# A 64-row last slot in two column halves of the array, and a scatter and a row request that come sooner

## The chip, the cores and the metric

The kernel runs on one core of one Trainium2 chip. The metric is the device time of one execution in microseconds (us), lower is better; the time shown for a kernel is the median of its timed runs. A profiled execution gives the trace from which the rows below come. "PE" is TensorE, "PEld" its weight loads, "DVE" VectorE, "ACT" ScalarE, "POOL" GpSimd, "SP" SyncE, which here issues nearly all transfers; a "q" behind a name (SPq, PEq) means the engine's sequencer.

## The reference

Sliding-window attention over q, k, v of shape 8 x 8 x 576 x 64 (batch, head, position, depth) with a window of 64, and behind it a mixture of 8 experts over the 4608 resulting rows of 512 numbers, each row going to the one expert that its logits choose:

```
scores = where(0 <= i - j < 64, q @ k.T / 8, -1e9);  x = softmax(scores) @ v      # per batch and head
logits = x @ w_gate + modality_bias[modality_id];    e = argmax(logits)            # per row, 8 experts
gate   = softmax(logits)[e]
out[row] = gate * (relu(x[row] @ w1[e]) @ w2[e])                                    # w1: 512x1024, w2: 1024x512
```

The inputs are float32. With the data of the benchmark three experts get rows: 1841, 2289 and 478.

## The kernel before

**Attention.** The 4608 rows are 36 pairs of two 64-row blocks. A loop over steps `s` runs four stages on different pairs: scores of pair `s` (64x64 tiles of the array, float32), the minima that mask and reduce them on DVE (`minima`, eight instructions with eight reads of the accumulator), exponentials on ACT (`exps`, split in groups of heads), transposes of the probabilities of pair `s-1` (`probs_t`), values of pair `s-2` (`values`, each float32 matmul a column half of the array: outputs on partitions 0 to 63 and 64 to 127), logits of pair `s-3`. The result of a pair goes into one of five buffers `xa` (512 numbers, the gate, the row's number). Transposes of q and k for the next group `G` of two pairs run in `part(0)` and `part(1)`; for some groups the upper four heads are loaded as 32x32 pieces (32x8x32 transfers) and turned on DVE instead of PE. DVE, ACT, POOL, SP and PE all execute in program order; the order is written out by hand.

**Routing.** Every second step a group's rows get a place in the scratch table `xs_scratch` in DRAM (`route1` to `route3`), in small DVE operations that wait in a list `routing` and are emitted a few at a time by `tick`. From group 4 on the last part (a cast of the indices, and per pair a copy of the row numbers on POOL and an indirect scatter of `xa`) is kept in `held` and emitted one step later by `release()`, which first empties `routing`.

**Experts.** Rows are worked off in slots of 256 rows of one expert. `slot_pieces` yields a slot in 16 pieces, and in the attention from step `FIRST` = 12 on each step interleaves four pieces (`gap`); behind the attention the pieces follow one another. A slot: `fetch` asks SP for the rows (`load_slot`, five transfers into the single buffer `xt`; SP waits there for the scatters that the slot needs), `x_turn` transposes them in 32x32 blocks on DVE, `x_part` splits each number into two reduced-precision parts (`xh`, `xl`), `first` makes the hidden layer from 3 products per term (`Whi*xh`, `Wlo*xh`, `Whi*xl`), `second` the output in the same way, `finish` multiplies by the gate and scatters the rows to `out`. Weights of an expert come in 16 pieces of 128x512 and are split into `Whi` (ACT) and `Wlo` (DVE).

**The end.** 18 whole slots are followed by one of at most 128 rows (one expert has 49 rows left over): `half_first` twice (12 matmuls of 512 columns each, 3 products), a transposition of the hidden layer and a split (`half_turn`) twice, `half_second` twice (24 matmuls of 256 columns each), with the last output pieces of the slot before in between. Then the two halves of its output are multiplied by the gate and scattered.

Of the kernel before, what the change touches and what calls it, by code (L numbers as in the profile page):

```python
# [19 lines left out]
P = 128  # L20
W64 = 64
# [5 lines left out]
def tile_window_attn_moe(  # L27
# [100 lines left out]

    def tick(n=1, table=False):
        for _ in range(n):  # L130
            if routing and not table:
                routing.pop(0)()
            elif queue:
                queue.pop(0)()
                issued[0] += 1
# [67 lines left out]
    def load_slot(row_ap, late, nb):  # L203
# [5 lines left out]
        parts.append((tail_of(xt)[:, 0:nb], rows[:, :, DM:ROW].rearrange("b p c -> p b c")))  # L209
        for dst, src in parts:  # L210
# [17 lines left out]

    todo = []
# [31 lines left out]
    def x_turn(sl):  # L261

        nb = sl["nb"]
        flat = sl["xt"].rearrange("p b c -> p (b c)")
        for b in range(nb):
            nc.vector.transpose(out=flat[:, b * DM:(b + 1) * DM], in_=flat[:, b * DM:(b + 1) * DM])  # L266

    def slot_pieces():


        def x_part(sl, i):

            xt, nb = sl["xt"], sl["nb"]
            if i == 0:
                sl["x"] = [epool.tile([P, NC1 * TP], F32R, name=nm) for nm in ("xh", "xl")]
                if nb == 1:
                    return
            cs_ = slice(2 * i, 2 * i + 2) if nb == 2 else slice(0, NC1)
            raw = x_of(xt)[:, 0:nb].rearrange("p b w c t -> p c (b w) t")[:, cs_]
            hi, lo = (x[:, cs_.start * nb * P:][:, 0:512].rearrange("p (c w t) -> p c w t", w=nb * NR, t=R32)  # L280
                      for x in sl["x"])

            def out_():
                split(raw, hi, lo)
                if i == 1:
                    sl["gate"] = epool.tile([P, 2], F32, name="gate", bufs=2)
                    nc.gpsimd.tensor_copy(out=sl["gate"][:, 0:nb], in_=tail_of(xt)[:, 0:nb, 0])
                    sl["id"] = epool.tile([P, 2], I32, name="id", bufs=2)
                    nc.gpsimd.tensor_copy(out=sl["id"][:, 0:nb], in_=tail_of(xt)[:, 0:nb, 1])
# [53 lines left out]
        def half_first(sl, n):  # L343

            buf = sl["buf"]
            hb = bank(n)
            hi, lo = sl["x"]
            mm = [(x, w, c) for c in range(NC1) for x, w in ((hi, Whi), (hi, Wlo), (lo, Whi))]
            for m, (x, w, c) in enumerate(mm):
                c0 = c * F + n * 512  # L350
                ready(sl, c0)
                nc.tensor.matmul(  # L352
                    out=hb, lhsT=x[:, c * P:(c + 1) * P], rhs=w[buf][:, c0:c0 + 512],
                    start=(m == 0), stop=(m == len(mm) - 1))
            hs = sl["hs", n] = work.tile([P, HP, P], F32, name="ss", bufs=3)
# [3 lines left out]
        def half_turn(sl, n):  # L359
            tp = bank(2)  # L360
            for c in range(HP):
                turn(tp[:, c * P:(c + 1) * P], sl["hs", n][:, c, :])
            hh = epool.tile([P, 512], F32R, name="hh", bufs=2)
            hl = epool.tile([P, 512], F32R, name="hl", bufs=2)
            sl["h", n] = hh, hl
            later.append(lambda: split(tp, hh, hl))

        def half_second(sl, a):

            buf = sl["buf"]  # L370
            cols = slice(a * DM // 2, (a + 1) * DM // 2)
            yp = ps_m.tile([P, DM], F32, name=f"y{a}")
            mm = [(w, n, c, lo) for n in range(2) for c in range(HP) for w, lo in ((Whi, 0), (Wlo, 0), (Whi, 1))]
            for m, (w, n, c, lo) in enumerate(mm):
                c0 = WC + (n * HP + c) * DM
                ready(sl, c0)
                nc.tensor.matmul(  # L377
                    out=yp[:, cols], lhsT=sl["h", n][lo][:, c * P:(c + 1) * P],
                    rhs=w[buf][:, c0 + cols.start:c0 + cols.stop],
                    start=(m == 0), stop=(m == len(mm) - 1))  # L380
            id2 = epool.tile([P, 1], I32, name=f"id{a}")
            nc.gpsimd.tensor_scalar(
                out=id2, in0=tail_of(sl["xt"])[:, 0, 1:2], scalar1=2.0, scalar2=float(a),
                op0=ALU.mult, op1=ALU.add)

            def out_():
                y = epool.tile([P, DM], F32, name="y", bufs=4)
                nc.vector.tensor_scalar(
                    out=y[:, 0:DM // 2], in0=yp[:, cols], scalar1=sl["gate"][:, 0:1], scalar2=None, op0=ALU.mult)
# [19 lines left out]
        while True:  # L409
            nxt = None  # L410
            for k in range(1, NK):
                for i in range(2):
                    if k == 1 and i == 0 and last:
                        nxt = fetch()
                        turn_at = 0
                    first(sl, k, i)
                    if k == NK - 1 and i == turn_at:
                        later.append(lambda: x_turn(nxt))
                    yield
                for t in range(2):  # L420
                    if k == 2 and t == 1 and nxt is None:
                        nxt = fetch()
                        turn_at = 1
                    second(sl, k - 1, t)
                    if k == NK - 1 and nxt and t == 1:
                        x_part(nxt, 1)
                    yield
                    if k == NK - 1 and nxt and t == 0:
                        x_part(nxt, 0)
                        run_later()  # L430
            second(sl, NK - 1, 0)
            yield
            if nxt["nb"] == 1:
                break
# [7 lines left out]
        half_first(nxt, 0)  # L442
        yield
        half_first(nxt, 1)
        yield
        half_turn(nxt, 0)
# [3 lines left out]
        half_turn(nxt, 1)  # L450
        yield
        half_second(nxt, 0)
        yield
        half_second(nxt, 1)
# [55 lines left out]
    QUARTERS = 8  # L510
# [42 lines left out]
    def quartered(G):  # L553

        return G >= QUARTERS and GBLK * G // BPB == (GBLK * G + GBLK - 1) // BPB

# [4 lines left out]
    def by_heads(t):  # L561
# [891 lines left out]
```

## Time and profile before

| | us |
|---|---|
| median of 3 timed runs | 620.34 (619.72 to 621.35) |
| profiled execution, its own time | 618.77 |
| its span, first to last instruction | 617.0 |
| PE busy | 596.8 |
| DVE busy | 389.0 |
| ACT busy | 292.7 |
| POOL busy | 139.2 |

The span is what the trace covers; the profiled execution's own time has 1.77 us around it. Its mean granted TensorE clock is 0.996 of full speed. "Busy" is the union of an engine's instructions; matmuls are pipelined, so their recorded durations overlap and the distance of two starts is what one costs.

### The profile page before, as it was taken

What the parts mean: (1) busy time and instruction counts of PE and PEld (TensorE: products, weight loads), DVE (VectorE), ACT (ScalarE), POOL (GpSimd) and SP (SyncE); (2) the same over time, 40 slices, a digit from 0 to 9 for tenths busy, and PEclk for the clock granted to TensorE, in tenths of its full rate; (3) what the DMA queues carried; (4) which work ended last, traced back from release to release, by engine and by line L of the source; (5) the groups of instructions that cost most, each with busy time, mean ns of one, the idle gap of its engine ahead of it and who ended that gap; (6) DMA issues with size and microseconds to landing.
All of it is one profiled execution on the core that took longest, in us unless ns stands there. A gap on an engine that the chain in (4) does not pass through costs nothing.

```text
span 617.0 us, 17344 instructions
## 1 busy us (share of the span) xinstructions
PE 596.8 (97%) x6309; PEld 534.2 (87%) x6309; DVE 389.0 (63%) x1493; ACT 292.7 (47%) x926; POOL 139.2 (23%) x315
## 2 busy tenths in 40 slices
PE   6999889999999999999999999999999999999996
PEld 4888778879898888988888899999999989999986
DVE  4899988877777877678655464323323834776622
ACT  3999885665656564646462111111112513554411
POOL 6323322132312311321223131001001101101202
PEclk9999999999999999999999999999999999999999
DMA  9989866685766745564413035522234534678300
GB/s 165 207 217 256 215 177 173 155 204 130 191 164 165 202 104 126 138 142 88 117 52 105 35 102 172 173 70 69 78 127 124 166 123 137 196 252 253 103 17 21
DMA packets 175111, 88.08 MB, mean 143 GB/s; under 512 B 138746, under 2 KB 157744, under 8 KB 174896
## 3 DMA queue, kind: packets, MB, share of 16 engines
q1 hardware_dynamic: 166400, 67.46, 44.8%
q0 software_dynamic: 5888, 18.93, 8.3%
q8 instruction: 50, 0.82, 0.6%
q10 hardware_dynamic: 2736, 0.58, 0.5%
q14 instruction: 37, 0.30, 0.2%
HBM read 67.49 MB, written 23.91 MB: 148 GB/s over the span
## 4 chain that ended last, share of the span: by engine, by line
PE 77%; DVE 5%; ACT 2%; issue 1%; DMA 1%; SPq 0%; POOL 0%; POOLq 0%; DVEq 0%; ACTq 0%
PE y L326 29%; PE em L304 21%; PE sp L304 10%; PE tp L470 7%; PE av L696 3%; PE sp L640 3%; PE tp L725 1%; DVE xt L266 1%; PE y L377 1%; DVE ss L654 1%; ACT ss L666 1%; DVE xl L196 1%; DMA xs_scratch<-xa,idx 1%; PE sp L352 0%; PE em L352 0%
## 5 line engine op out<-in xcount | busy, mean ns | idle before, releaser
L326 PE MATMUL y<-Whi,hh 128*128 128x512 f32 x288 | 115.7, 402 | 0.0
L666 ACT ACTIVATE ss<-ss,mn 128x128 f32<-128x128 f32 x288 | 112.3, 398 | 4.6 <-DVE less L159 3.7
L326 PE MATMUL y<-Wlo,hh 128*128 128x512 f32 x288 | 112.7, 391 | 0.0
L326 PE MATMUL y<-Whi,hl 128*128 128x512 f32 x288 | 112.4, 390 | 0.0
L337 POOL DMA_INDIRECT out_dram<-y,id x36 | 39.8, 1104 | 223.5 <-DVE y L334 161.3
L313 DVE SCALAR_TENSOR_TENSOR hl<-em,hh 128x512 fp32r<-128x512 f32 x50 | 34.5, 691 | 81.2 <-ACT hh L312 74.8
L304 PE MATMUL em<-xh,Whi 128*128 128x256 f32 x400 | 82.0, 286 | 0.0
L304 PE MATMUL em<-xh,Wlo 128*128 128x256 f32 x400 | 79.1, 279 | 0.0
L304 PE MATMUL em<-xl,Whi 128*128 128x256 f32 x400 | 79.1, 279 | 0.0
L312 ACT ACTIVATE hh<-em 128x512 fp32r<-128x512 f32 x50 | 29.9, 599 | 100.3 <-PE em L304 81.0
L675 ACT COPY pT<-tp 128x512 f32<-128x512 f32 x57 | 31.3, 589 | 78.6 <-PE tp L470 77.8
L654 DVE CUSTOM_DVE_ANT_0 ss<-sp,masks 128x128 f32<-128x128 f32 x288 | 63.6, 286 | 2.9 <-PE sp L640 2.0
L304 PEld LDWEIGHTS em<-xh,Whi 128*128 128x128 f32 x400 | 62.8, 188 | 2.6 <-issue 0.2
L326 PEld LDWEIGHTS y<-Whi,hl 128*128 128x128 f32 x288 | 54.1, 188 | 12.1
L326 PEld LDWEIGHTS y<-Whi,hh 128*128 128x128 f32 x288 | 54.1, 188 | 8.8
L326 PEld LDWEIGHTS y<-Wlo,hh 128*128 128x128 f32 x288 | 54.2, 188 | 8.5
L304 PEld LDWEIGHTS em<-xl,Whi 128*128 128x128 f32 x400 | 60.9, 188 | 0.0
L304 PEld LDWEIGHTS em<-xh,Wlo 128*128 128x128 f32 x400 | 60.9, 188 | 0.0
L809 POOL DMA_INDIRECT xs_scratch<-xa,idx x36 | 36.3, 1009 | 90.7 <-DVE e_n_p L154 30.6
L666 ACT ACTIVATION_READ_ACCUMULATOR ss<-ss,mn 128x1 f32 x288 | 56.1, 195 | 0.0
L312 ACT ACTIVATE hh<-sp 128x512 fp32r<-128x512 f32 x22 | 13.1, 597 | 76.2 <-PE sp L304 72.2
L696 PEld LDWEIGHTS av<-ve,pT 128*64 128x64 f32 x576 | 36.3, 138 | 12.6 <-issue 8.1
(242 smaller groups left out, 1194.4 us busy)
## 6 DMA issues: line engine op xcount, KB each, us to landing
xt<-xs_scratch SPq DMA_DIRECT2D x72, 128.0 KB
vo<-in_v_dram SPq DMA_DIRECT2D x32, 256.0 KB
y<-in_moe_w_dram SPq DMA_DIRECT2D x32, 256.0 KB
vo<-in_moe_w_dram SPq DMA_DIRECT2D x24, 256.0 KB
ss<-in_moe_w_dram SPq DMA_DIRECT2D x24, 256.0 KB
xs_scratch<-xs_scratch SPq DMA_DIRECT2D x8, 514.0 KB
pT<-in_moe_w_dram SPq DMA_DIRECT2D x16, 256.0 KB
qk<-in_k_dram SPq DMA_DIRECT2D x22, 128.0 KB
```

What stands on the lines that cost most here:

```text
L304: nc.tensor.matmul(out=hb[:, i * TP:(i + 1) * TP], lhsT=w[buf][:, c0:c0 + P], rhs=x[:, c * TP:(c + 1) * TP], start=(n == 0), stop=(n == le ...
L312: nc.scalar.activation(out=hh, in_=hb, func=AF.Relu),
L313: nc.vector.scalar_tensor_tensor(out=hl, in0=hb, scalar=0.0, in1=hh.bitcast(F32), op0=ALU.max, op1=ALU.subtract)))
L326: nc.tensor.matmul(out=sl["y", t], lhsT=h[:, i * TP + t * P:i * TP + (t + 1) * P], rhs=w[buf][:, c0:c0 + DM], start=(k == 0 and n == 0), s ...
L337: ins = nc.gpsimd.indirect_dma_start(out=out, out_offset=bass.IndirectOffsetOnAxis(ap=sl["id"][:, t:t + 1], axis=0), in_=y, in_offset=None ...
L470: nc.tensor.transpose(out=out_, in_=in_, identity=ident[p0:p0 + n, p0:p0 + n])
L640: nc.tensor.matmul(out=sp[a][c * W64:(c + 1) * W64, hp * P:(hp + 1) * P], lhsT=qT[rows, place(g + c, hp), :], rhs=kT[rows, win(c, hp), :], ...
L654: nc.vector.tensor_tensor_reduce(out=ss[a][:, hp, :], in0=sp[a][:, hp * P:(hp + 1) * P], in1=mask, scale=-1.0 / 8.0, scalar=3.0e38, op0=AL ...
L666: nc.scalar.activation(out=ss[a][:, hp, :], in_=ss[a][:, hp, :], func=AF.Exp, bias=mn[:, h:h + 1], scale=-1.0, accum_out=sm[:, h:h + 1])
L675: nc.scalar.copy(out=pT, in_=pp)
L696: nc.tensor.matmul(out=by_block(av)[c * W64:(c + 1) * W64, a, :, hp, :], lhsT=pT[:, i:i + W64], rhs=(vo if c else ve)[p][:, 2 * hp + a, :] ...
L809: ins = nc.gpsimd.indirect_dma_start(out=xs, out_offset=bass.IndirectOffsetOnAxis(ap=idx[:, j:j + 1], axis=0), in_=xg[j], in_offset=None)
```

## The change

The core of the diff:

```diff
@@ half slot @@
-        def half_first(sl, n):            # 12 matmuls of 128x512: x parts against Whi, Wlo
+        def half_first(sl):
+            hb = sl["hb"] = bank(0)
+            x = sl["xt"].rearrange("p b c -> p (b c)")
+            for c in range(NC1):
+                for n in range(2):
+                    c0 = c * F + n * 512
+                    nc.tensor.matmul(
+                        out=hb[n * W64:(n + 1) * W64], lhsT=x[:, c * W64:(c + 1) * W64], rhs=plain_w[c0 // WCH],
+                        start=(c == 0), stop=(c == NC1 - 1))
+        def half_second(sl):
+            yp = bank(2)[:, 0:DM // 2]
+            for m in range(NC2):
+                c, n = divmod(m, 2)
+                for a in range(2):
+                    c0 = WC + (n * HP + c) * DM
+                    nc.tensor.matmul(
+                        out=yp[a * W64:(a + 1) * W64], lhsT=sl["h"][:, c, n * W64:(n + 1) * W64],
+                        rhs=plain_w[c0 // WCH][:, a * DM // 2:(a + 1) * DM // 2], start=(m == 0), stop=(m == NC2 - 1))
@@ order of the end @@
-        half_first(nxt, 0); half_first(nxt, 1); half_turn(nxt, 0); second(sl, NK - 1, 1)
-        half_turn(nxt, 1); half_second(nxt, 0); half_second(nxt, 1)
+        half_first(nxt); second(sl, NK - 1, 0); half_turn(nxt); second(sl, NK - 1, 1); half_second(nxt)
@@ a slot's rows, in the attention @@
-                    if k == 2 and t == 1 and nxt is None:     # before second(sl, 1, 1)
-                        nxt = fetch()
-                        turn_at = 1
+                    if (k, i) == ((1, 0) if last else (2, 1)) and nxt is None:   # before first(sl, 2, 1)
+                        nxt = fetch()
-                    if k == NK - 1 and i == turn_at:
+                    if k == NK - 1 and i == 0:
                         later.append(lambda: x_turn(nxt))
@@ values_out @@
+        nc.gpsimd.tensor_copy(out=xa[:, DM + 1:DM + 2], in_=idc[:, p:p + 1])
@@ scatter @@
-            nc.gpsimd.tensor_copy(out=xg[j][:, DM + 1:DM + 2], in_=idc[:, p:p + 1])
+            nc.gpsimd.memset(pause, 0.0)
             ins = nc.gpsimd.indirect_dma_start(
@@ release @@
         if held:
-            tick(len(routing))
-            held.pop(0)()
+            ready_at, rows = held.pop(0)
+            assert done_routing[0] >= ready_at
+            rows()
@@ main loop @@
             minima(s)
+            if s > FIRST:
+                release()
...
             run_later()
-            release()
             tick(2)
...
-            for f, args in at.pop(s, ()):
-                f(*args)
+            loads(3)
...                                   # loads(1) behind part(0), loads(1) behind part(1), loads(9) at the end
```

The last slot holds at most 64 rows (the expert for it must have an odd number of 64-row blocks left). Its rows lie once per column half; its weights are loaded whole into 16 buffers of the finished attention (`plain_w`: `qT`, `xa`, `qk`, `ve`, `xaT`) and aren't split. `half_turn` transposes both halves at once, and its result goes to SBUF by a copy on ACT and one on DVE of 256 columns each. In the attention the transfers of q and k for one group are given out in parts over a step (`loads`), the plain heads first, the 32x8x32 ones later; which heads are loaded in which form stays as it was. From step 13 on, the held scatter stands directly behind the minima, and the rest of `routing` is no longer emptied there.

PE, at the end of the program (`em`, `sp`, `tp` and `y` are PSUM banks, `Whi`, `Wlo` the weight parts, `hh`, `hl` and `ss` the hidden layer). Before, from the last matmul of the second `half_first` into the first `half_second`:

```order
3227 L352 MATMUL sp_9459<-Whi_2524,xl 128x512
3228 L470 MATMUL tp<-ident_r,ss 128x128 x4
3229 L326 MATMUL y_9334<-Whi_65,hh 128x512
3230 L326 MATMUL y_9334<-Wlo_66,hh 128x512
3231 L326 MATMUL y_9334<-Whi_65,hl 128x512
3232 L326 MATMUL y_9334<-Whi_65,hh 128x512
3233 L326 MATMUL y_9334<-Wlo_66,hh 128x512
3234 L326 MATMUL y_9334<-Whi_65,hl 128x512
3235 L470 MATMUL tp<-ident_r,ss 128x128 x4
3236 L377 MATMUL y_9504<-Whi_2524,hh 128x256
3237 L377 MATMUL y_9504<-Wlo_67,hh 128x256
3238 L377 MATMUL y_9504<-Whi_2524,hl 128x256
```

The same place in the changed kernel, down to the last matmul:

```order
3208 L339 MATMUL y_9330<-Whi_65,hl 128x512
3209 L475 MATMUL tp<-ident_r,ss 128x128 x4
3210 L339 MATMUL y_9337<-Whi_65,hh 128x512
3211 L339 MATMUL y_9337<-Wlo_66,hh 128x512
3212 L339 MATMUL y_9337<-Whi_65,hl 128x512
3213 L339 MATMUL y_9337<-Whi_65,hh 128x512
3214 L339 MATMUL y_9337<-Wlo_66,hh 128x512
3215 L339 MATMUL y_9337<-Whi_65,hl 128x512
3216 L389 MATMUL tp<-xa_105,ss 64x256 x2
3217 L389 MATMUL tp<-qk,ss 64x256 x8
3218 L389 MATMUL tp<-ve,ss 64x256 x4
3219 L389 MATMUL tp<-xaT,ss 64x256 x2
```

24 matmuls of 128x512 (L352), 48 of 128x256 (L377) and 4 transposes are gone; 8 of 64x512 (L364, ahead of the output pieces shown) and 16 of 64x256 (L389) stand instead. Everywhere else PE's order is unchanged.

POOL, at steps 13 and 14 (`ve` and `rs` serve the values of a later step; `xa<-idc` is the copy of row numbers; the first scatter that is held). Before:

```order
103 L537 COPY ve<-vo 64x512
104 L681 TENSOR_SCALAR rs<-sm 128x8
105 L808 COPY xa_104<-idc 128x1
106 L809 DMA xs_scratch<-xa_104,idx 39168x514
107 L808 COPY xa_105<-idc 128x1
108 L809 DMA xs_scratch<-xa_105,idx 39168x514
109 L537 COPY ve<-vo 64x512
110 L681 TENSOR_SCALAR rs<-sm 128x8
```

Changed:

```order
113 L543 COPY ve<-vo 64x512
114 L692 TENSOR_SCALAR rs<-sm 128x8
115 L718 COPY xa_103<-idc 128x1
116 L819 MEMSET pause 1x1
117 L820 DMA xs_scratch<-xa_104,idx 39168x514
118 L819 MEMSET pause 1x1
119 L820 DMA xs_scratch<-xa_105,idx 39168x514
120 L543 COPY ve<-vo 64x512
121 L692 TENSOR_SCALAR rs<-sm 128x8
```

The copies of row numbers stand at the values of each step now, and a one-element memset stands ahead of each scatter.

DVE, at step 15, behind the minima (`xt` are the next slot's rows, `tgt` and `se` routing, `qT` the turned q, `hl` the hidden layer). Before:

```order
474 L543 COPY ve<-vo 64x512
475 L119 TENSOR_TENSOR Wlo_66<-y,Whi_65 128x512
476 L790 TENSOR_TENSOR tgt<-tp,ebase 128x16
477 L605 COPY qT<-tp 128x2x2x128
478 L313 SCALAR_TENSOR_TENSOR hl<-em,hh 128x512
479 L266 STREAM_TRANSPOSE xt<-xt 128x512 x2
480 L795 TENSOR_REDUCE se<-ex 128x2
```

Changed:

```order
474 L549 COPY ve<-vo 64x512
475 L279 STREAM_TRANSPOSE xt<-xt 128x512 x2
476 L119 TENSOR_TENSOR Wlo_66<-y,Whi_65 128x512
477 L802 TENSOR_TENSOR tgt<-tp,ebase 128x16
478 L616 COPY qT<-tp 128x2x2x128
479 L326 SCALAR_TENSOR_TENSOR hl<-em,hh 128x512
480 L807 TENSOR_REDUCE se<-ex 128x2
```

The two transposes of `xt` move ahead of four other operations. In step 14 the cast `idx<-dst` moves in the same way, from behind `ve` and six routing operations to directly behind the minima; ACT's small exponential of the routing (`ex`) moves behind three of the step's exponentials and the copy `xaT`. On SP, the request for `xt` moves ahead of the eight 32x8x32 transfers of q and of one or two weight transfers of its step.

## Rows read from the trace of the kernel before

**Rows 1.** The page: busy time of the engines (us, share of the span, instructions), and the granted TensorE clock in 40 slices of the span.

```profile
PE 596.8 (97%) x6309; PEld 534.2 (87%) x6309; DVE 389.0 (63%) x1493; ACT 292.7 (47%) x926; POOL 139.2 (23%) x315
PEclk9999999999999999999999999999999999999999
```

**Rows 2.** The waits of PE: line, who was waited for, us in total, times, longest.

```profile
PE tp L470 <- ACT pT L675: 3.1, 2, 1.9
PE av L696 <- POOL ve L537: 2.0, 4, 0.8
PE tp L470 <- DVE lg L730: 1.3, 3, 0.5
...
PE tp L470 <- ACT xaT L717: 0.4, 2, 0.2
```

**Rows 3.** The chain of work that ended last, from 594 us on: start, us, what.

```profile
594.07 4.11 PE y L326 x18
598.19 2.79 PE em L352 x12
600.98 2.79 PE sp L352 x12
603.78 0.44 PE tp L470 x4
604.21 1.40 PE y L326 x6
605.61 0.44 PE tp L470 x4
606.05 5.75 PE y L377 x48
611.83 0.50 DVE y L388
```

**Rows 4.** Timeline of PE where the values of one step begin and end (float32, column halves of 64): start, recorded us, line, operation, out<-moving,stationary, array rows*columns.

```profile
303.63 0.39 PE L326 MATMUL y<-Whi,hl 128*128 128x512 f32 x1
303.95 0.27 PE L696 MATMUL av<-ve,pT 128*64 128x64 f32 x1
...
304.06 0.22 PE L696 MATMUL av<-ve,pT 128*64 128x64 f32 x1
304.06 0.22 PE L696 MATMUL av<-vo,pT 128*64 128x64 f32 x1
304.11 0.22 PE L696 MATMUL av<-ve,pT 128*64 128x64 f32 x1
...
304.88 0.22 PE L696 MATMUL av<-vo,pT 128*64 128x64 f32 x1
```

**Rows 5.** Groups by line, weight loads: busy us, mean ns of one.

```profile
L326 PEld LDWEIGHTS y<-Wlo,hh 128*128 128x128 f32 x288 | 54.2, 188 | 8.5
L696 PEld LDWEIGHTS av<-vo,pT 128*64 128x64 f32 x576 | 36.3, 138 | 0.0
```

**Rows 6.** Busy time of each engine in stretches: the attention ahead of the slots, and the slots behind the attention (us, instructions; then clock, DMA share, GB/s).

```profile
15.00:72.00 57.00, 52.39 (x1006) 47.06 (x1003) 51.91 (x286) 53.56 (x213) 20.91 (x40) 0.98 0.95 225
334.00:596.00 262.00, 261.99 (x1717) 238.24 (x1718) 127.22 (x271) 74.68 (x136) 36.10 (x78) 1.00 0.42 130
```

**Rows 7.** Timelines of DVE, POOL and ACT: an output scatter that has a memset ahead of it, a held scatter that has a copy ahead of it, and the first copy of the last slot's hidden layer.

```profile
598.23 0.75 DVE L334 TENSOR_SCALAR y<-y,gate 128x512 f32<-128x512 f32 x1 [2.19 <-PE y L326]
...
599.26 0.99 POOL L337 DMA_INDIRECT out_dram<-y,id  x1 [13.67 <-DVE y L334]
...
101.21 0.16 DVE L821 CAST idx<-dst 128x2 int32<-128x2 f32 x1
...
102.15 1.06 POOL L809 DMA_INDIRECT xs_scratch<-xa,idx  x1 [7.60 <-DVE Wlo L119]
...
103.69 0.97 POOL L809 DMA_INDIRECT xs_scratch<-xa,idx  x1 [0.28 <-issue]
...
601.02 0.60 ACT L356 ACTIVATE ss<-em 128x512 f32<-128x512 f32 x1 [5.80 <-PE em L352]
```

**Rows 8.** Timelines of POOL and PE around 43 us: the copy `ve` behind a pair of scatters, and the values that wait for it.

```profile
43.02 0.62 POOL L537 COPY ve<-vo 64x512 f32<-64x512 f32 x1
...
43.70 0.27 PE L696 MATMUL av<-ve,pT 128*64 128x64 f32 x1 [0.75 <-POOL ve L537]
```

**Rows 9.** Steps 14 and 15: the scatter and the row request as pieces of the chain (start, us, what), and SP's queue (start, us to issue).

```profile
103.69 4.12 DMA xs_scratch<-xa,idx
...
110.89 1.86 DMA xt<-xs_scratch
...
97.79 5.07 SPq L590 DMA_DIRECT2D qk<-in_q_dram  x8
...
108.35 2.95 SPq L211 DMA_DIRECT2D xt<-xs_scratch  x5
```

**Rows 10.** Timelines of DVE and PE from step 14 to 16.

```profile
99.64 0.42 DVE L543 COPY ve<-vo 64x512 f32<-64x512 f32 x1
...
109.86 0.42 DVE L543 COPY ve<-vo 64x512 f32<-64x512 f32 x1
...
111.71 0.17 DVE L790 TENSOR_TENSOR tgt<-tp,ebase 128x16 f32<-128x16 f32 x1 [0.71 <-PE tp L780]
...
113.99 1.30 DVE L266 STREAM_TRANSPOSE xt<-xt 128x512 f32<-128x512 f32 x2
...
116.30 0.71 DVE L568 STREAM_TRANSPOSE qT<-qk 128x512 f32<-128x512 f32 x1
...
118.92 0.66 PE L470 MATMUL tp<-ident_r,ss 128*128 128x128 f32 x4 [0.45 <-DVE lg L730]
```

**Rows 11.** Timelines of ACT and PE: at step 20 the routing's exponential and the wait of a transpose, and behind "..." a wait of PE near the end of the attention.

```profile
165.32 0.22 ACT L756 ACTIVATE ex<-lg 128x16 f32<-128x16 f32 x1 [2.00 <-DVE lg L753]
...
167.22 0.66 PE L470 MATMUL tp<-ident_r,qk 128*128 128x128 f32 x4 [0.22 <-ACT xaT L717]
...
325.75 0.66 PE L470 MATMUL tp<-ident_r,ss 128*128 128x128 f32 x4 [0.40 <-DVE lg L730]
```

More of the change, by code (lines that the diff above doesn't have):

```diff
@@ L341, in finish @@
             tc.add_to_no_dep_group("outs", ins.ins)
-        def half_first(sl, n):
[L345 to L355, printed above, removed]
+        def half_first(sl):
[4 more added lines that the diff above has]
+                    c0 = c * F + n * 512
+                    ready(sl, c0)
+                    nc.tensor.matmul(
+                        out=hb[n * W64:(n + 1) * W64], lhsT=x[:, c * W64:(c + 1) * W64], rhs=plain_w[c0 // WCH],
+                        start=(c == 0), stop=(c == NC1 - 1))
+            hs = sl["hs"] = work.tile([P, HP, P], F32, name="ss", bufs=3)
@@ L368, in half_second @@
[L368 to L381, printed above, removed]
+                turn(tp[:, c * P:(c + 1) * P], sl["hs"][:, c, :])
@@ new lines, in half_turn @@
+            hT = sl["h"] = work.tile([P, HP, P], F32, name="ss", bufs=3)
+            flat = hT.rearrange("p c f -> p (c f)")
+            later.append(lambda: (
+                nc.scalar.copy(out=flat[:, 0:TP], in_=tp[:, 0:TP]),
+                nc.vector.tensor_copy(out=flat[:, TP:2 * TP], in_=tp[:, TP:2 * TP])))
+        def half_second(sl):
[4 more added lines that the diff above has]
+                    c0 = WC + (n * HP + c) * DM
+                    ready(sl, c0)
+                    nc.tensor.matmul(
+                        out=yp[a * W64:(a + 1) * W64], lhsT=sl["h"][:, c, n * W64:(n + 1) * W64],
+                        rhs=plain_w[c0 // WCH][:, a * DM // 2:(a + 1) * DM // 2], start=(m == 0), stop=(m == NC2 - 1))
+            id2 = epool.tile([P, 1], I32, name="id0")
+            upper = epool.tile([P, 1], F32, name="upper")
@@ L589, in load_qk @@
                     src = x[b, h, g * W64:(g + n) * W64, c * R32:(c + 1) * R32]
-                    dma.dma_start(out=by_heads(t)[rows, (h - nh) // 2, u, :],
-                                  in_=src.rearrange("(u p) d -> p u d", p=R32))
+                    other = nh == 0 and h % 2 and c
+                    (nc.scalar if other else dma).dma_start(
+                        out=by_heads(t, nh)[rows, (h - nh) // 2, u, :],
+                        in_=src.rearrange("(u p) d -> p u d", p=R32))
             i += n
     def heads_t(G, nm, i, tp):
-        src = plain(qk[G, nm], HP if quartered(G) else H).rearrange("p t (h a) d -> p t h (a d)", a=2)
+        src = plain(qk[G, nm], n_plain(G)).rearrange("p t (h a) d -> p t h (a d)", a=2)
         for h in range(2):
@@ L770, in route2 @@
     def route2(G, tp):
-        while routing:
-            routing.pop(0)()
+        tick(len(routing))
         oh = chosen[G]
@@ L824, in rows @@
             scattered.append(f"scatter_after_{G}")
-        (held if G >= HOLD else routing).append(rows)
+        if G >= HOLD:
+            held.append((done_routing[0] + len(routing), rows))
+        else:
+            routing.append(rows)
     def counts(G, tp):
@@ L898, in tile_window_attn_moe @@
             when(step, new_qk, G, nm)
-            when(step, load_qk, G, nm)
+            for h in (0, *range(max(n_plain(G), 2), H, 2)) if n_plain(G) < H else (0,):
+                when(step, load_qk, G, nm, range(GBLK), nc.sync, range(h, h + 2))
     pieces = []
@@ L1069, in tile_window_attn_moe, with loads @@
         R = (s - 5) // GB if s >= 5 and j == 1 else -1
+        def loads(n):
+            for f, args in at.get(s, [])[:n]:
+                f(*args)
+            at[s] = at.get(s, [])[n:]
         def part(i):
@@ L1158, in tile_window_attn_moe @@
             tick(n_tick)
+            loads(1)
             if s < NPR:
@@ L1167, in tile_window_attn_moe @@
         tick(n_tick)
+        if s > FIRST:
+            loads(1)
         if s == WEIGHTS:
@@ L1171, in tile_window_attn_moe @@
             weights(s)
+        if s > FIRST:
+            loads(9)
         if n_gap > 3:
@@ L1301, in tile_window_attn_moe @@
     ahead = []
+    flat = qT.rearrange("p c i -> p (c i)")
+    plain_w.extend(flat[:, n * WCH:(n + 1) * WCH] for n in range(4))
+    plain_w.extend(x[:, 0:WCH] for x in xas)
+    for _ in range(2):
+        t = work.tile([P, 2, H, D], F32, name="qk", bufs=2).rearrange("p t h d -> p (t h d)")
+        plain_w.extend(t[:, n * WCH:(n + 1) * WCH] for n in range(2))
+        plain_w.append(work.tile([P, H, D], F32, name="ve", bufs=2).rearrange("p h d -> p (h d)"))
+    plain_w.append(work.tile([P, DM], F32, name="xaT"))
+    assert len(plain_w) == 2 * WC // WCH
     waited = 0
@@ L1321, in tile_window_attn_moe @@
         if swaps and swaps[0][0] <= t:
-            swaps.pop(0)
-            split_hi(*ahead[0])
-            split_lo(*ahead.pop(0))
-    assert not swaps and not todo
+            x = swaps.pop(0)[2]
+            raw, buf, c = ahead.pop(0)
+            if x == NANY:
+                load_piece(plain_w[c], ea[x], c)
+            else:
+                split_hi(raw, buf, c)
+                split_lo(raw, buf, c)
+    assert not swaps and not todo and not held
     manual.__exit__(None, None, None)
```

102 lines of the change are left out of this document (58 added, 44 removed).

## The prediction

> **What bounds the kernel now.** I read the page first: PE is busy 596.8 of 617.0 us, no other engine above 63%, and its granted clock has a 9 in every slice [rows 1]. So only what PE executes, and the 20 us in which it stands, can shorten the run. The waits of PE say who it stood for [rows 2]: a few short ones each for ACT, POOL and DVE. The busy times by stretch say where [rows 6]: behind the attention (334 to 596) PE has 261.99 of 262.00 us, so there nothing but removed matmul time counts; from 15 to 72, ahead of the slots, it has 52.39 of 57.00, with ACT at 53.56, DVE at 51.91 and the transfer engines at 0.95. Last the chain: from 594 us on it is PE alone until 611.80, then the last output's multiplication, its scatter and the end of the program, about 5.2 us [rows 3]. These stay as they are.
>
> **The end.** Removed from the chain are the two first halves, 2.79 + 2.79, one of two turns, 0.44, and the second half, 5.75 [rows 3]: 11.77 us. The output pieces (1.40 each) and one turn remain. Added are 8 matmuls of 64x512 and 16 of 64x256 in full precision. No row before has this shape. The nearest are the values `av`: full precision, moving data 64 columns wide, outputs in two column halves. A float32 matmul is two passes there (16 matmuls of a step leave 32 records: 576 + 576 in 36 steps [rows 5]). A pass of the upper half starts with one of the lower half, both at 304.06, and from there to 304.88 the pairs follow every 0.82 / 14 = 0.0586 us (16 pairs, the first of them at 303.95) [rows 4]. In proportion, 512 columns are 0.469 us a pair. The first layer has 16 passes, 8 pairs: 3.75 us; the second 32 passes of 256, 16 pairs at 0.234: 3.75 us. Together 7.5, an upper end if some of the 0.0586 is the same for any width. The nearest wide row is a reduced-precision pass, 2.79 / 12 = 0.2325 us for 512 columns [rows 3]; two of its kind would be 0.465, the same price, and if a tenth of the 0.0586 were fixed (an estimate), some 6.8 would be the lower end. I take 7.2. Each change between the whole array and halves costs something: a last whole matmul of 512 columns at 303.63 is followed by `av` after 0.32 us instead of 0.233 [rows 4], so 0.09, three times: 0.27. The end gains 11.77 - 7.2 - 0.27 = **4.3** (4.0 to 4.7).
>
> What covers the rest of it: the first Relu, 0.60 us on ACT [rows 7], runs beside the output pieces of 1.40 that stand between the first layer and the turn. The two copies behind the turn (256 columns each) run beside the next 1.40; DVE's stands behind a multiplication `y` of 0.75 [rows 7] and so just fits. Without this cover some 0.5 us would show. The splits of the last weights, gone from ACT and DVE, gain nothing, as PE stands 0.01 us in that stretch [rows 6]; so do the ten row transfers in place of five, which are asked a slot ahead. The whole copies of the weights need buffers of the finished attention and arrive during that stretch too, where the transfer engines have a share of 0.42 [rows 6].
>
> **The steps with slots.** Here PE stands 0.45 at 118.92 for `lg` [rows 10], 0.22 at 167.22 and once more (0.4 in two) for ACT's `xaT` [rows 2, 11], and 0.40 at 325.75 for `lg` [rows 11]: 1.27 together. For `xaT` the cause is in the rows: ACT stood 2.00 us in the routing's exponential `ex`, which waits for DVE's logits [rows 11], and `xaT` was queued behind it. The change puts `ex` behind `xaT`. For `lg` DVE's order is the cause: in step 15 it did `Wlo`, `tgt`, `hl` and the 1.30 of the `xt` transposes late, from 113.99 to 115.29, then `qT` at 116.30 [rows 10]. Now the transposes come directly behind `ve`.
>
> Does `xt` arrive by then? Before, the cast of the indices ended at 101.37 and a scatter started at 102.15, with 0.78 between for the copy and a semaphore; the second started at 103.69, landed 4.12 later, SP issued the rows from 108.35 over 2.95, and the last landed at 112.75 [rows 7, 9]. Now the cast stands behind the minima, at about 99.7, where `ve` was (99.64 [rows 10]). With a memset ahead, a scatter starts 0.28 behind what it waited for (598.23 + 0.75 to 599.26 [rows 7]). So the first starts at 100.1 to 100.5, the second 1.3 to 1.5 later, 101.4 to 102.0, about 2 us sooner, and the last row lands at about 110.5 to 111.1. DVE reaches the transposes at 109.86 + 0.42 = 110.28 [rows 10]: it waits 0.2 to 0.8. Queued behind are `Wlo`, `tgt`, `qT` and `hl`, but DVE had a hole of 0.71 ahead of `tgt` [rows 10], which takes this up. What is late next is q: its eight 32x8x32 transfers, 5.07 of SP's time [rows 9], now go out behind `xt`, until about 114.5, and the last should land some 1.86 later (as `xt` [rows 9]) at 116.4, against 116.30, when DVE turned `qT` [rows 10]. So part of the 0.45 may stay. POOL's `ve` and `rs` stand behind both scatters, and are done by about 104, a step ahead of the values that need them. Of 1.27 I take **1.0** (0 to 1.27).
>
> **Ahead of the slots.** The values waited for POOL's `ve` four times, 2.0 in all [rows 2], 0.75 of it at 43.70, behind a pair of scatters [rows 8]. A scatter starts 0.78 - 0.28 = 0.5 sooner behind its indices, and the copy between the two is gone (103.69 - 102.15 = 1.54 from start to start [rows 7], about 1.35 without its 0.2), so a pair ends 0.7 to 0.9 sooner. Against it, a copy of 0.2 is added at the values of every step. At most 2.0 - 4 x 0.11 = 1.57 comes back, at worst 0.2 is lost. With ACT busy 53.56 and DVE 51.91 of 57.00 and transfers at 0.95 [rows 6], what PE no longer waits for here it may wait for elsewhere: I take **0.5**.
>
> **Sum.** 4.3 + 1.0 + 0.5 = 5.8. The profiled execution's own time, 618.77 (span 617.0 and 1.77 around it), would become 613.0. It lies 1.57 below the median of 620.34; the median would become **614.5**.
>
> **Rivals.**
>
> *The end alone gains.* The waits of PE shift to the next late thing (q in step 16, ACT ahead of the slots). For it: ACT and DVE are nearly full there [rows 6]. Time: 620.34 - 4.3 = 616.0.
>
> *The column halves take turns* when 512 wide. Then 24 pairs become 48 passes, 15 instead of 7.5, and the end loses 3.5. With 1.5 from the rest: 622.3. If only one layer did so, the end would gain 0.55, and the total 618.3. Against it: both halves start at the same 304.06 [rows 4], though those columns are few.
>
> *Weight loads in the way.* Each pass has a load, 138 ns for 64 columns [rows 5]. If the 48 loads stood between the passes instead of beside them, they would cost 6.6, the end would lose 2.3, and with the rest's 1.5 the time would be 621.1. Rows against it: in `av` pairs follow every 0.0586, less than one load's 0.138, and in the wide matmuls loads of 0.188 [rows 5] lie under a distance of 0.2325. The Trainium skill, "TensorE: Matmul & The Clock Gate", Part 3: Packing small matmuls, "The mechanism", says that a weight load overlaps with matmuls under way only when its group of rows differs; both halves here use the same 128 rows, so by it this rival would hold. The rows just named disagree with it.
>
> *Late rows hold up the slots* (the one on the slower side). DVE works in order, and the `xt` transposes now stand ahead of `Wlo`, `tgt`, `qT` and `hl`. If the rows land at 112.75 as before, DVE waits 112.75 - 110.28 = 2.47, less 0.71 of hole: 1.76 at such a slot. Slots are fetched every fourth step from 14 on, the earliest behind the freshest scatters; at three slots this loses 5.3 of the 5.8, and the time is 619.8. Over 622.2 (a loss of 7.7) it comes when three slots lose 2.6 each, with rows landing at 113.6, or six lose 1.3 each, with rows at 112.3. For it: SP gives out transfers in order and five row transfers take it 2.95. Against it: the scatter that SP waits for comes 2 us sooner.
>
> **How the numbers follow.** Chances: the forecast 0.68; the end alone 0.15; halves in turn 0.04 and loads in the way 0.04; late rows 0.05; something else 0.04. A measurement tells about 0.3%, 1.86 us, from no change: below 618.5 is faster, above 622.2 slower. Forecast and the end alone are faster, with a part of the others: 0.86. In between: the loads, half of the turns and of late rows: 0.08. Slower: 0.06. The forecast's bounds are 620.34 - (4.7 + 1.27 + 1.57) = 612.8 and 620.34 - (4.0 + 0 - 0.2) = 616.5. Below, up to 1.3 more comes if one of the two waits for `pT` (3.1 together, the longest 1.9 [rows 2]), which the order doesn't explain, goes away: 611.5. Above, one slot with late rows at half of 1.76 is added to the end alone: 617.4.
>
> **What the changed kernel's profile would show.** The end: 8 pairs of 64x512 passes about 0.45 apart and 16 of 64x256 about 0.225 apart, both halves starting together; from the first layer's start to the last matmul 2.8 + 0.44 + 7.2 + 0.27 = 10.7 us, where before the same work took 13.6 and a piece of 1.40 that stood ahead of it; PE not waiting for the Relu or the copies. In step 15: `xt` landed before 111.2, DVE waiting under 0.8 ahead of its transposes. PE's waits for `xaT` gone, for `lg` down from three to one or two, for POOL's `ve` at about 1 or less. The prediction is wrong if pairs are 0.6 us or more apart, if DVE stands over 1 us ahead of the transposes in several steps, or if the last slot's first matmul starts less than 0.5 sooner than before while the end gains.

## The result and the profile of the changed kernel

The changed kernel takes **623.6 us** (median of 10, 621.5 to 625.6), the kernel before, in all its runs of the same session, 619.75 (617.6 to 621.4). The ratio is 1.0065 (1.0051 to 1.008): 4 us slower, where 5.8 faster was forecast. The profiled execution has a span of 622.5 us; before, 617.0. The page (PE's busy time and the granted clock, to be held against [rows 1]) and the waits of PE in the whole run (us, times, longest; against [rows 2]):

```profile
PE 598.0 (96%) x6281; PEld 531.0 (85%) x6281; DVE 375.6 (60%) x1479; ACT 281.7 (45%) x907; POOL 138.8 (22%) x349
PEclk7999989999999899999999999999999999999999
```

```profile
PE sp L651 <- DVE qT L577: 1.7, 2, 1.4
PE tp L737 <- ACT xaT L729: 1.6, 2, 1.1
PE tp L475 <- DVE tgt L802: 1.2, 2, 0.9
PE tp L475 <- DVE lg L742: 1.2, 2, 0.6
...
PE av L707 <- POOL ve L543: 0.9, 1, 0.9
```

PE runs 28 matmul records fewer and is yet busy 1.2 us longer: in three slices the clock is below full. The wait for `ve` has fallen from 2.0 to 0.9 as forecast, but waits for DVE's `qT` and `tgt` stand there that the kernel before doesn't have, and those for `xaT` are 1.6 us where [rows 2] has 0.4. The end of the chain, against [rows 3]:

```profile
606.71 3.58 PE em L364 x16
610.29 1.57 PE y L339 x6
...
613.68 3.63 PE tp L389 x32
```

The first layer takes 3.58 us, the second 3.63; from the first layer to the last matmul it is 10.60 us, where before the same work took 13.61 and a piece of 1.40. **The end gained 4.4 us**, and the loss lies ahead of it. Where, the first `values` matmul of step 13 and that of step 37 (the last) tell. Of before and of the changed kernel, in two fences:

```profile
83.59 0.27 PE L696 MATMUL av<-ve,pT 128*64 128x64 f32 x1
...
332.37 0.27 PE L696 MATMUL av<-ve,pT 128*64 128x64 f32 x1
```

```profile
87.62 0.27 PE L707 MATMUL av<-ve,pT 128*64 128x64 f32 x1
...
342.67 0.27 PE L707 MATMUL av<-ve,pT 128*64 128x64 f32 x1
```

From step 13 to 37 the kernel before takes 248.78 us, the changed one 255.05: **6.3 us lost in the steps with slots**. `loads_once` (below) takes 247.79 there (84.26 to 332.05). The later start of step 13 (83.6 before, 87.6 changed) lies within what one trace differs from another: the changed kernel's instructions up to there reached it at 84.3 in `loads_once`, and at 82.1 in `release_late`. So these traces don't show whether the change did anything ahead of step 13. With 4.0 here, 6.3 and the shorter end (4.4, and 0.4 in the stretch before it) the spans add up: 4.0 + 6.3 - 4.8 = 5.5.

**One step shows the loss.** 4.8 of the 6.3 us lie in step 24. SP's queue over steps 22 and 23 (start, us to issue), first before, then changed:

```profile
181.98 3.96 SPq L590 DMA_DIRECT2D qk<-in_q_dram  x8
186.19 0.37 SPq L107 DMA_DIRECT2D y<-in_moe_w_dram  x1
191.99 2.44 SPq L211 DMA_DIRECT2D xt<-xs_scratch  x5
```

```profile
186.31 1.58 SPq L593 DMA_DIRECT2D qk<-in_q_dram  x2
196.37 2.51 SPq L220 DMA_DIRECT2D xt<-xs_scratch  x5
198.93 4.46 SPq L600 DMA_DIRECT2D qk<-in_q_dram  x8
203.64 0.99 SPq L107 DMA_DIRECT2D y<-in_moe_w_dram  x2
```

Before, SP gave out q's eight 32x8x32 transfers and a weight piece, and only then stood at the row request (186.6 to 191.99). Now the request comes first. SP stands at it from 187.9 (186.31 + 1.58) to 196.37, for the row table that DVE computes and for the scatter, with nothing to do meanwhile; q's transfers take 4.46 behind it, and the next weight piece goes out at 203.64. What SP waited for at the requests of this stretch (90 to 230 us, three slots): `rows` is the row table, `xs_scratch<-xa,idx` a scatter. First before, then changed, then `loads_once`:

```profile
SPq L211 <- DMA xs_scratch<-xa,idx: 3.4, 3, 1.4
SPq L204 <- DVE rows L142: 3.2, 1, 3.2
```

```profile
SPq L207 <- DVE rows L145: 14.1, 3, 5.2
...
SPq L220 <- DMA xs_scratch<-xa,idx: 7.3, 5, 2.0
```

```profile
SPq L207 <- DVE rows L145: 1.0, 2, 0.6
```

For the scatters SP waits 7.5 us in `loads_once`, about as long as in the changed kernel.

In the changed kernel ACT pays for it at each of the three slots, 11.1 us together (waits of ACT from 100 us on); before, it has no wait for a weight piece:

```profile
ACT Whi L114 <- DMA y<-in_moe_w_dram: 11.1, 3, 5.2
```

What the late weight piece does in step 24, in the timelines of ACT, DVE and PE:

```profile
207.73 0.62 ACT L114 CAST Whi<-y 128x512 fp32r<-128x512 f32 x1 [5.17 <-DMA y<-in_moe_w_dram]
208.26 0.58 ACT L729 COPY xaT<-tp 128x512 f32<-128x512 f32 x1
208.74 0.60 ACT L325 ACTIVATE hh<-em 128x512 fp32r<-128x512 f32 x1
...
209.37 0.69 DVE L326 SCALAR_TENSOR_TENSOR hl<-em,hh 128x512 fp32r<-128x512 f32 x1 [4.68 <-ACT hh L325]
...
210.75 0.71 DVE L577 STREAM_TRANSPOSE qT<-qk 128x512 f32<-128x512 f32 x1 [0.15 <-DMA qk<-in_k_dram]
...
208.89 0.64 PE L737 MATMUL tp<-wg,xaT 128*64 128x8 f32 x16 [1.10 <-ACT xaT L729]
211.51 0.67 PE L651 MATMUL sp<-kT,qT 64*64 64x128 f32 x16 [1.39 <-DVE qT L577]
213.37 1.11 PE L475 MATMUL tp<-ident_r,ss 128*128 128x128 f32 x4 [0.60 <-DVE lg L742]
```

ACT stands 5.17 us for the weight piece; `xaT` and `hh` are queued behind it on ACT; on DVE `hl` waits for `hh`, and `qT` comes 1.38 us behind the start of `hl`, its input 0.15 late at most; PE waits three times, 3.1 us. Then the clock: the busy times of 214 to 217 (the last three numbers are the granted clock, the transfer engines' share and GB/s) and two matmuls in it:

```profile
214.00:217.00 3.00, 3.00 (x11) 2.46 (x10) 2.39 (x19) 2.48 (x11) 0.75 (x1) 0.54 0.83 213
```

```profile
214.71 0.63 PE L339 MATMUL y<-Wlo,hh 128*128 128x512 f32 x1
215.13 0.63 PE L339 MATMUL y<-Whi,hl 128*128 128x512 f32 x1
```

The granted clock is 0.54, near the lower level of 1.2 GHz, and matmuls of 512 columns follow every 0.43 us instead of 0.23: some 1.5 us more (an estimate). The other low digits of the page's row lie in the first slice and in that of 78 to 93 us, ahead of step 13 or at its start.

### The profile page after: what moved, and what is told of

It is laid out like the page before. It is cut to its first block, busy times and chain, and to the rows that moved or that the text cites. A ratio compares the mean times of both kernels' runs of the same rounds, so it can differ in the third digit from the quotient of the medians.

```text
span 622.5 us, 17279 instructions
## 1 busy us (share of the span) xinstructions
PE 598.0 (96%) x6281; PEld 531.0 (85%) x6281; DVE 375.6 (60%) x1479; ACT 281.7 (45%) x907; POOL 138.8 (22%) x349
## 4 chain that ended last, share of the span: by engine, by line
PE 80%; DVE 3%; DMA 2%; issue 1%; SPq 1%; ACT 1%; POOL 0%; POOLq 0%; DVEq 0%; ACTq 0%
PE y L339 30%; PE em L317 22%; PE sp L317 10%; PE tp L475 8%; PE av L707 4%; PE sp L651 3%; PE tp L737 2%; DMA qk<-in_k_dram 1%; DMA xt<-xs_scratch 1%; PE tp L389 1%; DVE ss L665 1%; PE em L364 1%; DVE Wlo L119 0%; SPq L593 0%; SPq L535 0%
## 5 line engine op out<-in xcount | busy, mean ns | idle before, releaser
L820 POOL DMA_INDIRECT xs_scratch<-xa,idx x36 | 37.7, 1047 | 178.8 <-DVE idx L832 142.5
```

Of the source, the lines that this page charges most:

```text
L820: ins = nc.gpsimd.indirect_dma_start(out=xs, out_offset=bass.IndirectOffsetOnAxis(ap=idx[:, j:j + 1], axis=0), in_=xg[j], in_offset=None)
```

## The experiments

All are the changed kernel with an edit; the ratios are to the kernel before, with 95% intervals.

**1. `end_only`:** only the last slot is changed, all else as before.

> The changed last slot alone; loads, row request, release, copies and memsets as before. The trace of the changed kernel has its attention (start of the values of pair 35) 10.3 us later than before and its end 4.8 us shorter. If the two are independent, this kernel takes 619.75 - 4.8 = 615.0 us (614 to 616). Rival: the new slot itself disturbs the attention (its longer table of the plan on DVE, other buffers): over 618 us.

Measured: 614.49 us, **0.9943** (0.9924 to 0.9963). The end alone gains 3.5 us (2.3 to 4.7); the loss is all in the other edits.

**2. `fetch_late`:** the row request back by two pieces, and DVE's transposes of the rows back with it (`turn_at`).

```diff
-                    if (k, i) == ((1, 0) if last else (2, 1)) and nxt is None:
+                    if k == 1 and i == 0 and last:
                         nxt = fetch()
+                        turn_at = 0
...
-                    if k == NK - 1 and i == 0:
+                    if k == NK - 1 and i == turn_at:
...
+                    if k == 2 and t == 1 and nxt is None:
+                        nxt = fetch()
+                        turn_at = 1
                     second(sl, k - 1, t)
```

> The changed kernel, only the request for a slot's rows (and its turn on DVE) back where it was. Theory 'SP is held': at step 23 the request, two pieces sooner, stood from 188 to 196 us on SP waiting for the slot's row table and for the scatter, and q's pieces and a weight piece behind it came late; ACT waited 5.2 us for that piece and PE 1.3 and 1.6 us behind ACT and DVE, then ran some 3 us at half clock. By it most of the 10 us goes: 615 to 619 us. Rival 'scatter behind the minima': 622 to 624. Rival 'loads in parts': 622 to 624.

Measured: 614.11, **0.9933** (0.9909 to 0.9957).

**3. `loads_once`:** the request stays sooner, q and k are asked at once.

```diff
-            loads(3)
+            loads(99)
             gap(it, True)
```

> The changed kernel, only the transfers of q and k for a group given out at once as before. Theory 'SP is held': q's pieces come before the held request again, the weight piece still behind it, so a part comes back: 619 to 622 us. Rival 'loads in parts' (q and k late by being split): 615 to 618. Rival 'scatter behind the minima': 622 to 624.

Measured: 613.86, **0.9939** (0.9918 to 0.9961). Either edit undone takes the whole loss away: it is the two together that cost. I had expected a part. SP's queue and ACT in `loads_once` show why nothing is left (the weight piece behind the request goes out at 193.5, and ACT doesn't wait for it; over the three slots ACT waits 1.5 us for weight pieces, 11.1 in the changed kernel):

```profile
182.22 3.96 SPq L600 DMA_DIRECT2D qk<-in_q_dram  x8
190.78 2.48 SPq L220 DMA_DIRECT2D xt<-xs_scratch  x5
193.51 0.96 SPq L107 DMA_DIRECT2D y<-in_moe_w_dram  x2
```

```profile
196.78 0.62 ACT L114 CAST Whi<-y 128x512 fp32r<-128x512 f32 x1
```

**4. `release_late`:** the scatter back behind the gap, the rest of the routing emptied ahead of it.

> The changed kernel, only the held scatter back behind the gap, with the routing emptied ahead of it as before (memset and early copies stay). Theory 'SP is held': the request waits even longer for its scatter: 623 to 626 us. Rival 'scatter behind the minima' (POOL's and ACT's order is the cause): 615 to 619.

Measured: 625.28, **1.0116** (1.0091 to 1.0141). SP waits for the scatters longer (10.9 us from 90 to 230 us, 7.3 in the changed kernel) and the loss grows. The scatter's new place helps against the held request; it isn't the cause.

**5. `q_last`:** behind a held request the weight piece goes out ahead of q's transfers.

```diff
             tick(n_tick)
-            loads(1)
...
-        if s > FIRST:
-            loads(1)
```

> The changed kernel (623.6 us), only the 32x8x32 transfers of q and k now all behind the step's weight transfers instead of between them: behind a held row request SP gives out the weight piece about 4 us sooner and the q pieces later. Theory 'late weights' (ACT stands for the weight piece, and the transposes' copies behind it make PE wait): 614 to 618 us. Rival 'late q' (DVE stands for q's pieces and PE for the turned q): 624 to 628 us.

Measured: 620.23, **1.0023** (1.0005 to 1.004): between the two, so a part comes back, and less than 'late weights' expected. The edit doesn't take the weights' lateness away: ACT still waits 10.0 us for weight pieces, in five waits of at most 2.8 (11.1 in three, at most 5.2, in the changed kernel). In its profiled execution PE no longer waits for `xaT` or `qT` from step 13 on; in step 15 the rows came late instead, and the step takes 4.8 us longer than before (timelines of DVE and PE):

```profile
113.50 1.30 DVE L279 STREAM_TRANSPOSE xt<-xt 128x512 f32<-128x512 f32 x2 [3.03 <-DMA xt<-xs_scratch]
...
115.52 0.65 PE L475 MATMUL tp<-ident_r,qk 128*128 128x128 f32 x4 [2.95 <-DVE tgt L802]
```

This is the rival "late rows" of the prediction, in one of its slots.

**6. and 7. `extra_8`, `extra_4`:** `loads_once` plus eight, or four, transfers behind the row request of steps 14, 18 and 22, that nothing waits for.

```diff
+        if extra[0]:                       # in steps 14, 18, 22
+            for n in range(8):             # 4 in extra_4
+                nc.sync.dma_start(
+                    out=ex_dram[extra[1]], in_=q[0, n % H, 0:4 * W64, 0:R32].rearrange("(u p) d -> p u d", p=R32))
+                extra[1] += 1
```

> The kernel with the transfers given out at once (613.9 us), plus eight transfers of q's form (256 rows of 32 numbers, into a scratch in DRAM that nothing reads) directly behind the row requests of steps 14, 18 and 22. q itself is as early as there; only the weight pieces behind the request come some 4 us later. Theory 'late weights': 619 to 624 us. Rival 'late q': 613 to 615 us.

> As the kernel with eight extra transfers behind three row requests (1.46% over before, 13 us over the one without them), with four instead: the weight pieces come about 2 us later instead of 4 to 5. If the loss follows the delay: half of it, 619 to 621 us. If there is slack for the first 2 us: 613.5 to 616.

Measured: `extra_8` 627.83, **1.0146** (1.0121 to 1.0172); `extra_4` 620.35, **1.0027** (1.0003 to 1.0051). Above `loads_once` that is 2.1 and 0.9%, 13 and 5.5 us: the loss grows with the time for which SP is kept from the weight pieces, though q is as early as in `loads_once`. SP's queue of `extra_8` at step 23, ACT, and PE's two waits:

```profile
203.05 5.17 SPq L227 DMA_DIRECT2D extra_scratch<-in_q_dram  x8
208.48 1.00 SPq L108 DMA_DIRECT2D y<-in_moe_w_dram  x2
```

```profile
211.93 0.62 ACT L115 CAST Whi<-y 128x512 fp32r<-128x512 f32 x1 [5.05 <-DMA y<-in_moe_w_dram]
...
213.08 0.64 PE L744 MATMUL tp<-wg,xaT 128*64 128x8 f32 x16 [0.99 <-ACT xaT L736]
215.52 0.67 PE L658 MATMUL sp<-kT,qT 64*64 64x128 f32 x16 [1.20 <-DVE qT L584]
```

The same picture as in the changed kernel, made by 5.17 us of SP's time alone; here too `hl` and `qT` follow ACT, and q has long landed. `extra_4` shows this path less clearly: ACT waits for a weight piece at each slot (9.1 us in three), but PE's largest wait in its trace is another, 2.3 us for `lg` in step 17, where DVE stands 3.48 us for an output scatter (see `both_back`), and rows are late too (1.4 us of PE for `tgt`).

**8. `copy_back`:** the copies of row numbers back ahead of each scatter, no memset.

> The changed kernel, only the copies of the row numbers back ahead of each scatter on POOL and the memset gone. By the prediction the stretch ahead of the slots loses 0.5 us: 624.1 us. If the copies don't matter: 623.6. If the added copies of each step delay POOL's ve and rs: under 622.5.

Measured: 626.69, **1.0116** (1.0086 to 1.0146). None of the three: 3 us worse than the changed kernel. The scatter starts later, and in its trace SP stands 17.7 us for the row table and 8.9 for the scatters (14.1 and 7.3 above); DVE stands 9.5 us for output scatters (3.9 in the changed kernel).

**9. `release_loads_once`:** edits 3 and 4 together.

> Transfers given out at once and the held scatter back behind the gap, row request two pieces sooner. Against the kernel with only the transfers at once (613.9 us): by the prediction's 1.0 us for the order of the steps with slots 614.9; if the scatter's place does not matter, 613.9; if the sooner request needs the sooner scatter (SP stands longer for it, with the weights behind): 616 to 620.

Measured: 619.93, **1.0001** (0.9977 to 1.0025), with runs from 614 to 625. Without the sooner scatter, the sooner request costs some 4 us even with q ahead of it. Its trace shows the rival "late rows" at all three slots: DVE waits 2.38, 1.89 and 2.65 us for the rows ahead of its transposes, and PE about as long behind it.

**10. `both_back`:** edits 2 and 3 together: SP's order and the place of the transposes are those of `end_only`, the scatter, memset and copies are the changed ones.

> The changed kernel with the row request and the transfers of q and k back where they were: SP's order is that of the kernel with the new end alone; the scatter behind the minima, the memset and the early copies stay. The prediction gave the order of the steps with slots 1.0 us and the stretch ahead of them 0.5: by it 1.5 us under the kernel with the new end alone (614.5), 613.0. If these edits gain nothing by themselves: 614.0 to 615.0.

Measured: 613.80, **0.9927** (0.9902 to 0.9951), against 0.9943 (0.9924 to 0.9963) of `end_only`: the intervals overlap, so a gain of 1 us from these edits is neither shown nor excluded. `both_back`, `fetch_late` and `loads_once` beat both kernels and can't be told apart.

The trace of `both_back` shows why these edits bring so little. From step 13 to 37 it takes 248.80 us, no less than before (248.78), `end_only` 247.11. On POOL the held scatters, now directly behind the minima, stand ahead of a slot's output scatter, which before came first. POOL before, then POOL and DVE in `both_back`:

```profile
122.93 1.05 POOL L337 DMA_INDIRECT out_dram<-y,id  x1 [5.10 <-DVE lg L753]
...
124.75 0.98 POOL L809 DMA_INDIRECT xs_scratch<-xa,idx  x1 [0.55 <-POOL xa L808]
```

```profile
122.38 0.97 POOL L824 DMA_INDIRECT xs_scratch<-xa,idx  x1 [0.21 <-issue]
...
124.61 1.06 POOL L350 DMA_INDIRECT out_dram<-y,id  x1 [0.17 <-issue]
...
129.51 0.75 DVE L347 TENSOR_SCALAR y<-y,gate 128x512 f32<-128x512 f32 x1 [3.20 <-DMA out_dram<-y,id]
```

DVE stands for the later output scatter before it can scale the slot's next output, and `lg` is queued behind that: PE waits 4.2 us for `lg` in `both_back`, 0.8 before (from 90 us on). DVE has such waits in the slots of all nine traces with the scatter behind the minima and in none of the five without, `end_only` and `release_late` among them.

**11. and 12. `turn_late`, `turn_late_2`:** DVE's transposes of the rows back behind `hl`, in the changed kernel and in experiment 9.

```diff
-                    if k == NK - 1 and i == 0:
+                    if k == NK - 1 and i == (0 if last else 1):
                         later.append(lambda: x_turn(nxt))
```

> The changed kernel (1.0065 of before), only DVE's two transposes of a slot's rows back behind hl, where they stood before; SP's order stays. Theory 'late weights' alone: the weight pieces are as late, so nothing comes back: 622 to 625 us. Theory 'late rows' (DVE stands ahead of the transposes with tgt and qT behind it) as the larger part: 614 to 617 us. If both take part: between.

> The kernel with transfers at once and the scatter back behind the gap (1.0001 of before, runs from 614 to 625 us), with DVE's transposes of the rows back behind hl as well. In its trace DVE stood 2.4 us ahead of the transposes in step 15 and PE 4.1 us for tgt in two places. If 'late rows' is what costs and scatters there: 614 to 616 us, with a narrow spread. If not: 618 to 621, with the same spread.

Measured: `turn_late` 627.74, **1.015** (1.0129 to 1.017); `turn_late_2` 621.21, **1.0037** (1.0023 to 1.0051), with a narrow spread. The first is worse by 5 us; the second by 2, with intervals that just touch. In the changed kernel "late rows" isn't the larger part: its trace has one such wait of DVE, 1.0 us in step 19, and PE's 1.2 us for `tgt`. The longest group among the waits of PE from 90 us on in `turn_late`:

```profile
PE sp L651 <- DVE qT L577: 6.5, 3, 2.6
```

None for `tgt` is left, and those for `qT` come to four times as much: `hl` waits for the late `hh`, and now 1.30 us of transposes stand between it and `qT`. So the edit removes one wait and lengthens another, and its time doesn't give the price of late rows.

## Why the prediction was wrong, and where it was right

**Right: the end.** 7.2 us for the two layers, measured 3.58 + 3.63 = 7.21; from the first layer on 10.7, measured 10.60; the gain 4.3, measured 4.4 in the trace and 3.5 (2.3 to 4.7) in `end_only`. The price of `av` in proportion to the columns (0.469 us a pair of 512) holds within a tenth. The loads of the first layer, two at a time, one for each half:

```profile
607.12 0.14 PEld L364 LDWEIGHTS em<-qT,xt 128*64 128x64 f32 x2 [0.29 <-issue]
607.55 0.14 PEld L364 LDWEIGHTS em<-qT,xt 128*64 128x64 f32 x2 [0.29 <-issue]
```

A pair comes every 0.43 us, with its two loads under the passes. So both rivals of the end fall: halves in turn would have taken 15 us by the prediction's price, and loads between the passes 6.6 more. That 7.2 is met to 0.01 is partly luck: eight pairs at 0.43 are 3.4 us, half of the forecast's lower end of 6.8, and the rest of the 3.58 lies at the changes to and from whole-array matmuls, which had 0.27 of their own in the sum. For that rule of the Trainium skill's page "TensorE: Matmul & The Clock Gate" (Part 3: Packing small matmuls, "The mechanism"), that a load overlaps with matmuls under way only where the group of rows differs, this trace disagrees too: all passes here use the same 128 rows, and loads of 0.14 us lie under pairs 0.43 apart.

**Partly right, and worth little: the waits it named.** POOL's `ve` went from 2.0 to 0.9 us, and ACT's `ex` no longer stands ahead of `xaT`. But PE's waits for `xaT` aren't gone (1.6 us in two, before 0.4; the longer, 1.1, comes from the weight piece of step 24), and those for `lg` went from 1.3 to 1.2 only. Ahead of the slots 0.5 was taken; no run here shows it, as `both_back` lies 1 us below `end_only` within the intervals.

**Right: the scatter and the rows of step 15.** The changed kernel's step 15 starts 3.13 us later than before's (first `values` matmul at 108.31 against 105.18). Timelines of POOL, DVE and ACT:

```profile
104.54 0.97 POOL L820 DMA_INDIRECT xs_scratch<-xa,idx  x1 [0.21 <-issue]
...
113.58 1.31 DVE L279 STREAM_TRANSPOSE xt<-xt 128x512 f32<-128x512 f32 x2
...
116.90 0.62 ACT L114 CAST Whi<-y 128x512 fp32r<-128x512 f32 x1 [2.31 <-DMA y<-in_moe_w_dram]
```

Less 3.13, the second scatter starts at 101.4 (forecast 101.4 to 102.0), and DVE turns the rows at 110.45 without a wait (forecast 110.28 and a wait of 0.2 to 0.8).

**The step that failed: "what is late next is q".** There I followed q's eight transfers behind the row request, priced them, and stopped. Behind q on the same queue stood weight pieces, as the order of SP shown with the change said ("ahead of one or two weight transfers"), and I gave them no cost. ACT waits 2.31 us for one in step 15 already, 5.17 in step 24, and 11.1 over the three slots. And the request's own wait on SP had no price in my sum: it is held about 8.5 us at the slot shown above, 21.4 over the three, mostly for the row table of the plan on DVE. Before, q's transfers and a weight piece went out first and SP stood 6.6 us over the three slots, and ACT never waited for a weight piece; the sooner request made idle time of SP out of what q's transfers had filled. So the term of +1.0 for the steps with slots was -6.3 in the trace (and, together with the 0.5 ahead of the slots, -7.5 from `end_only` to the changed kernel by the medians, 0.9943 to 1.0065). One of the prediction's own signs of being wrong came true with it: the last slot's first matmul starts at 606.71, 8.5 us later than before (598.19), while the end gains. POOL's queue was followed no further either: `ve` and `rs` behind the two scatters were looked at, the output scatter behind them was not (`both_back`).

**The rival on the slower side** had the place (three slots, the request that holds up a queue) but the wrong victim: DVE standing for rows. That occurred, with one wait of 1.0 us in the changed kernel, one of 3.03 in `q_last` and one at every slot of `release_loads_once`, but in the changed kernel it isn't the main part. Late weight pieces are enough for a loss of this kind (`extra_8`), and in step 24 they are what ACT waits for. Its bound, five transfers of 2.95 us, left out that the request can stand for the row table. That the clock would fall behind waits that add up was in no case of mine; it is some 1.5 of the 4.8 us of step 24.

**Open:** how the 6.3 us split between late weights, late q and late rows. `q_last` gets back a third of the loss by weights ahead of q, but its profiled execution loses 4.8 us in the step with the late rows, so it doesn't settle the shares. `both_back` isn't faster than `end_only` by the forecast's 1.5; its trace names the later output scatter, but no run with that scatter put ahead again shows what it costs.

## What to carry to other kernels

In this kernel a request that must wait for a semaphore does best behind what is ready on its queue: moved ahead of it, the wait became idle time of the queue. Follow the queue to the end of the step, not to the next item: the victim here was the third in line, on another engine. And two edits that are each harmless can cost together, so cost them as one order of the queue.

## What the runs showed of the hardware

Full-precision matmuls in two column halves keep nearly the price per column of `av` up to 512 columns: a pair of passes of 512 comes every 0.43 us (3.58 us for eight pairs), of 256 at 0.227 (3.63 for sixteen), with loads of the same rows beside them. A transfer of 256 rows of 32 numbers costs SP 0.5 to 0.65 us to issue (3.96 to 5.07 for eight into SBUF, 5.17 for eight from DRAM to DRAM), more than a weight piece of 128x512 (0.37). Three waits of PE of 1.10, 1.39 and 0.60 us within 6 us were followed by some 3 us at a granted clock near one half.
